# Forty-five column-reordering copies moved from GpSimd to ScalarE, with a newly written instruction order

## The chip, the cores and the metric

The kernel runs on one core of a Trainium2 chip. The metric is the device time of one execution in microseconds (us). The kernel before took 771.58 us as the median of three runs, which lay between 764.45 and 779.27 us.

A core has five instruction queues that run beside each other and meet only at semaphores: TensorE (PE in the profile, with its weight loads as PEld), VectorE (DVE), ScalarE (ACT), GpSimd (POOL) and SyncE (SP), which here does nothing but issue DMA transfers. Each queue runs its instructions strictly in the order in which they were written.

## The reference

Two blocks follow each other. The first is a linear-attention recurrence over 768 steps, for 4 batches of 8 heads with 40 channels each; the second is a dense layer pair over the resulting 3072 tokens, with an activation h·cos(h) between the two products.

```python
def _attn_ref(r, k, v, w, a, b):
    ...
    for t in range(S):
        ...
        y[:, :, t] = np.einsum('bhd,bhde->bhe', rt, state)
        Sa = np.einsum('bhde,bhe->bhd', state, at)
        state_decay = state * wt[:, :, None, :] - np.einsum('bhd,bhe->bhde', Sa, bt)
        state = state_decay + np.einsum('bhd,bhe->bhde', vt, kt)

def _moe_ref(x, w_in, w_out):          # x: 3072 x 320, w_in: 320 x 2048
    h = x @ w_in
    g = h * np.cos(h)
    return (g @ w_out).astype(np.float32)
```

## The kernel before

**Attention.** The 768 steps are cut into 24 chunks of 32 steps. Within a chunk the recurrence is turned into small matrix products plus the inverse of a triangular 32x32 matrix per batch and head. Four chunks share one inversion, so there are six inversions ("quads" 0 to 5). An inversion is a run of short VectorE steps: for quads 2 to 5 each step j is one multiply into `inv_tmp` (line 655) and one subtract into `inv` (line 659), 31 steps a quad; it starts with a transpose into `u` (line 647) and ends with a transpose into `rt` (line 663). The state is carried from chunk to chunk through the tokens t, q, x, s and z (functions `ch_t` to `ch_z`); in `ch_z` VectorE adds the products to the state `qz` (line 916) and GpSimd multiplies it by the decay (line 917).

**Dense layers.** Finished chunks are joined in pairs to 12 groups of 256 tokens. For each group and each of four blocks j of the inner dimension, `first_a` and `first_b` fill two PSUM tiles `ph` with x·w_in. For each of the two, ScalarE rounds (line 1000), VectorE subtracts (line 1002), ScalarE takes the absolute value and the sine (lines 1006, 1007) and VectorE multiplies (line 1010). From group 3 on the second product is done with seven instead of eight block products: small sums on GpSimd (`s`, lines 1082 and 1090) and VectorE (lines 1084, 1086), then `seven`.

**The copies.** The operands r, v, a and w are wanted with the channels on the partitions. For early chunks TensorE transposes them. From quad 3 on for w, and from quad 2 on for a, r and v, it is done by way of DRAM: `quad_fetch` (line 277) brings four chunks of one operand into the tile `ws` with four DMAs; for w, VectorE then forms running products in place (lines 357 and 362); `quad_turn` (line 291) copies the columns of `ws` from the order (t, d) to (d, t) in three parts of 14, 13 and 13 channels, that is 448, 416 and 416 elements a partition; `quad_store` (line 298) writes each part to DRAM; `turned_load` (line 322) reads it back with the channels on the partitions. There are 15 such operands (four each of a, r and v, three of w), so 45 copies. There is one `ws`, so the next fetch waits for the third copy of the operand before. The copies' targets are two buffers used in turn (`nat_a`), so a copy also waits until the store of the part two before it has landed.

**Order.** Nothing is scheduled automatically. The string `PLAN` holds 1,536 tokens, each the name of a function above and its arguments, and the instructions are emitted in that order; each queue gets its part of it. `rf:a:3` is the fetch of operand a for quad 3 (for w the token is `sf:3`, and `sc:3` and `ss:3` are its running product and the store of it), `pt:a:3:1` the copy of its part 1, `st:a:3:1` the store of that part, `lt:12:a` the load of chunk 12. `ij:12:20` is step 20 of the inversion of the quad that starts at chunk 12, `fa:g:j` and `fb:g:j` are the first product of group g and block j, `y:g:j:n` the rest of its activation. `L:c:n:q:h` are the first loads with the queue that issues them (s, a or p for SyncE, ScalarE or GpSimd). `B:n` and `K:n` put in n matmuls on a zero tile.

Of the kernel before, what the change touches and what calls it, by code (L numbers as in the profile page):

```python
# [17 lines left out]
L:1:a:p:l L:2:w:s:l L:0:w:a:r L:0:b:p:r L:1:b:s:r L:0:v:p:r B:4 L:0:a:p:r B:5 B:3 L:3:w:s:r L:1:w:s:l  # L18
L:1:w:a:r L:0:w:s:l L:3:b:p:r L:2:b:s:r L:3:w:s:l L:0:a:s:l L:0:k:s:r L:3:a:s:r L:1:a:p:r L:0:b:p:l L:2:b:s:l
pw:0 L:2:w:s:r L:2:a:p:r L:0:r:s:r L:1:b:s:l L:2:a:p:l pa:0 L:3:b:p:l pw:2 L:3:a:s:l pa:2 sp:0 sf:1 pb:0 pn:0  # L20
L:0:k:s:l sc:1 pb:2 pn:2 lo:2 L:0:v:s:l B:4 lo:0 kn:0 is:0 wf:1 L:0:r:s:l in:0 L:1:r:p:l L:1:k:p:r L:1:k:s:l
ip:0:15 wt:1 ip:0:14 ld:5:a ip:0:13 ip:0:12 ip:0:11 ip:0:10 ip:0:9 k:0 L:1:r:s:r v:0 L:1:v:p:l B:2 ip:0:8
ip:0:7 ip:0:6 g:0 ip:0:5 ip:0:4 L:1:v:s:r wf:0 B:4 wf:2 kn:1 k:1 in:1 B:3 v:1 L:2:r:s:r ip:0:3 ip:0:2 x:0 g:1
ip:0:1 L:2:v:s:r wt:2 L:2:k:p:r wm:1 wg:1 it:0 L:2:v:s:l ss:1 wp:1 ih:0 F:0:0:0 S:0:0:0 wm:2 wg:2 wf:3 wt:3
ld:4:w wp:2 wf:4 s:0 L:2:r:p:l K:6 ld:5:w wg:3 wt:0 wm:0 B:4 wf:6 wg:0 in:2 z:0 L:2:k:s:l kn:2 B:5 wm:3 wp:3
L:3:v:p:l B:4 wf:7 F:0:1:0 t:1 B:5 L:3:v:p:r wp:0 K:14 wt:4 wm:4 F:0:2:0 L:3:k:p:r wt:6 wm:6 q:1 L:3:r:s:l
wf:8 wg:4 wp:4 wt:7 k:2 wm:7 wf:9 wg:6 wp:6 wg:7 B:4 L:3:r:s:r wp:7 S:0:1:0 wf:10 K:6 x:1 wt:8 B:3 B:3 wt:9
wm:9 L:3:k:p:l wf:5 s:1 B:4 v:2 wm:8 wg:9 wp:9 g:2 wg:8 wp:8 B:6 tk:0 wt:10 wm:10 z:1 wg:10 wp:10 B:6 t:2 q:2
wf:11 wf:12 wt:11 tk:1 K:4 wf:13 wm:11 wt:5 wm:5 wg:5 wp:5 kn:3 B:3 S:0:2:0 wg:11 k:3 wp:11 wt:13 wm:13 B:6
x:2 tb:0 in:3 v:3 wg:13 wt:12 wm:12 wp:13 tb:1 wg:12 wf:14 wt:14 K:6 wp:12 fa:0:0 fb:0:0 y:0:0:0 y:0:0:1 wg:14  # L30
y:0:0:2 wm:14 s:2 K:29 wf:16 wf:15 ld:4:r g:3 wp:14 fa:0:1 fb:0:1 ld:4:b wf:17 F:0:3:1 wt:15 wm:15 wg:15 r:4
sd:0:0:0 z:2 y:0:1:1 ld:5:b sd:0:0:1 K:13 y:0:1:0 y:0:1:2 S:0:3:1 sf:2 ld:4:v wt:16 wm:16 ld:4:a ld:6:b t:3
K:20 r:5 wp:15 wf:18 sc:2 wg:16 sd:0:1:1 pw:4 ld:7:w fa:0:2 q:3 wp:16 fb:0:2 y:0:2:0 pa:4 ld:6:w wf:19 y:0:2:1
in:4 ld:4:k kn:4 tk:2 wt:17 wm:17 x:3 pb:4 y:0:2:2 sd:0:1:0 wg:17 ss:2 s:3 ld:7:b sd:0:2:1 wp:17 wt:18 wm:18
wt:19 wm:19 ld:5:k wg:19 fa:0:3 r:7 ld:6:a r:6 pn:4 lo:4 pw:6 fb:0:3 z:3 pb:6 y:0:3:0 ld:7:a pa:6 rf:a:2
y:0:3:2 wg:18 sp:4 pn:6 sd:0:2:0 wp:18 is:4 ip:4:15 lo:6 ld:5:r v:4 pt:a:2:1 y:0:3:1 wp:19 k:4 ip:4:14 t:4 g:4
ip:4:13 ip:4:12 ip:4:11 tb:2 ip:4:10 ip:4:9 ip:4:8 pt:a:2:0 ip:4:7 tk:3 ip:4:6 ip:4:5 ip:4:4 ld:5:v in:5
sd:0:3:0 kn:5 k:5 q:4 ip:4:3 ip:4:2 v:5 tb:3 fa:1:0 g:5 st:a:2:0 pt:a:2:2 ld:9:w rf:r:2 ip:4:1 fb:1:0 y:1:0:0
st:a:2:1 pt:r:2:1 T:1:0 x:4 sd:0:3:1 st:a:2:2 y:1:0:1 pt:r:2:0 it:4 F:4:0:1 y:1:0:2 F:4:1:1 sd:1:0:0 ld:9:b
ld:8:w lt:8:a ld:8:b ih:4 S:4:0:1 st:r:2:0 s:4 st:r:2:1 r:9 lt:9:a ld:6:k fa:1:1 pw:8 xa:8 ld:11:w ld:6:v r:8  # L40
ld:10:w fb:1:1 z:4 kn:6 ld:11:b T:0:0 sd:1:0:1 y:1:1:1 pb:8 y:1:1:0 y:1:1:2 F:4:3:1 pt:r:2:2 rf:v:2 st:r:2:2
ld:6:r F:4:2:1 t:5 fa:1:2 tk:4 lt:10:a S:4:1:1 q:5 ld:10:b fb:1:2 xa:9 in:6 y:1:2:0 ld:7:k x:5 lt:11:a
sd:1:1:0 s:5 k:6 pt:v:2:0 r:11 sp:8 y:1:2:1 sd:1:1:1 pt:v:2:1 pn:8 y:1:2:2 sd:1:2:1 z:5 o:0:0 ld:7:v tk:5
fa:1:3 v:6 pw:10 xa:10 st:v:2:0 pt:v:2:2 tb:4 g:6 r:10 fb:1:3 ld:7:r in:7 y:1:3:0 y:1:3:1 S:4:3:1 xa:11
sd:1:2:0 tb:5 pb:10 S:4:2:1 y:1:3:2 o:0:1 pn:10 is:8 sf:3 t:6 ij:8:31 fa:2:0 sc:3 kn:7 k:7 q:6 v:7 ij:8:30
st:v:2:2 fb:2:0 y:2:0:1 x:6 sd:1:3:0 sd:1:3:1 ij:8:29 ij:8:28 ij:8:27 ij:8:26 st:v:2:1 ss:3 y:2:0:0 lt:8:r
ld:12:b y:2:0:2 ij:8:25 ld:12:w ld:13:w s:6 pt:w:3:0 st:w:3:0 lt:8:v fa:2:1 fb:2:1 z:6 y:2:1:1 ij:8:24
sd:2:0:0 sd:2:0:1 T:0:1 y:2:1:0 y:2:1:2 T:3:0 o:1:0 r:12 tk:6 g:7 ld:8:v ld:8:k ij:8:23 ij:8:22 t:7 fa:2:2
ij:8:21 q:7 o:1:1 pt:w:3:2 fb:2:2 x:7 T:0:2 T:0:3 y:2:2:1 lt:9:r pt:w:3:1 st:w:3:2 ij:8:20 ij:8:19 y:2:2:0
kn:8 y:2:2:2 sd:2:1:0 k:8 st:w:3:1 s:7 ld:9:k sd:2:1:1 ij:8:18 ij:8:17 ij:8:16 z:7 ij:8:15 ij:8:14 rf:a:3  # L50
# [78 lines left out]
def kernel(  # L129
# [43 lines left out]
    nc = tc.nc  # L173
# [1057 lines left out]
```

## Time and profile before

| | |
|---|---|
| median of three runs | 771.58 us |
| profiled execution, its own time | 774.15 us |
| its span, first to last instruction | 772.4 us |
| mean granted clock of TensorE | 0.971 |
| moved by DMA | 78.12 MB, 101 GB/s on average |

The profile is that of one execution, and the prediction's sum starts from that execution's own time: 772.4 us of span and 1.75 us around it. An engine's busy time is the time in which one of its instructions ran. A row of the groups names the line, the engine, the operation, the tiles written and read, the shape and the count; then stand the busy time of the group in us and the mean of one in ns; then the time that the engine sat idle just before these instructions, with what ended most of it. The chain of waits is followed back from the last instruction to what released each one; its shares tell which engine the time went through.

### The profile page before, as it was taken

To read this page: it belongs to the slowest core of one execution; us is meant where nothing else is said; L and a number is where in the kernel's file an instruction comes from. 1 tells how busy PE (TensorE), PEld (TensorE's weight loads), DVE (VectorE), ACT (ScalarE), POOL (GpSimd) and SP (SyncE) were. 2 spreads that over 40 slices of the span, in tenths; PEclk is the share of its full clock that TensorE was granted. 3 is DMA by queue.
4 is the path that set the end of the run, shared out by engine and by line. 5 is a ranking of instruction groups with operands and counts; after the bars stand their busy time and mean duration, and the time that the engine had idled before them with its cause. 6 is when DMAs were issued, how large, how long until landed. Compare 5 with 4: busy or idle time off the path is not lost.

```text
span 772.4 us, 40189 instructions
## 1 busy us (share of the span) xinstructions
PE 713.3 (92%) x17948; PEld 586.3 (76%) x17948; DVE 558.7 (72%) x1199; ACT 359.3 (47%) x719; POOL 291.3 (38%) x468
## 2 busy tenths in 40 slices
PE   4758999999989998999998999999999999999995
PEld 2645678777777776888877888887888888888885
DVE  5989889896346898387998768898647895454342
ACT  1335565754544534354444454535445445554432
POOL 8625303333340553463463442532624313231211
PEclk9869999999998998999999999999999999999998
DMA  8576564565555368446567566556633221211000
GB/s 129 103 178 170 148 174 100 133 122 87 109 125 114 74 129 140 95 93 138 96 134 132 120 129 128 122 121 105 131 76 68 53 58 48 49 27 30 21 18 18
DMA packets 268541, 78.12 MB, mean 101 GB/s; under 512 B 230128, under 2 KB 261872, under 8 KB 268368
## 3 DMA queue, kind: packets, MB, share of 16 engines
q1 hardware_dynamic: 266064, 73.82, 46.0%
q8 instruction: 141, 2.31, 1.3%
q0 software_dynamic: 1216, 1.56, 1.1%
q10 hardware_dynamic: 1088, 0.16, 0.1%
q14 instruction: 32, 0.26, 0.1%
HBM read 54.53 MB, written 20.97 MB: 98 GB/s over the span
## 4 chain that ended last, share of the span: by engine, by line
PE 64%; DVE 22%; ACT 5%; issue 4%; SPq 2%; POOL 2%; DMA 1%; DVEq 0%; POOLq 0%
PE ph L210 22%; PE po L210 15%; PE dps L210 4%; DVE inv L659 3%; PE x0ps L210 3%; DVE inv_tmp L655 3%; PE p L210 2%; PE sps L210 2%; PE gram L210 2%; PE busy L210 2%; DVE turns L1002 2%; PE qps L210 2%; PE nps L210 2%; PE sT L807 1%; DVE gT L1010 1%
## 5 line engine op out<-in xcount | busy, mean ns | idle before, releaser
L210 PE MATMUL ph<-xT,w_in_sb 128*128 128x256 f32 x768 | 186.4, 389 | 2.6 <-DVE gT L1010 2.0
L210 PEld LDWEIGHTS ph<-xT,w_in_sb 128*128 128x128 f32 x768 | 141.6, 192 | 31.4 <-issue 12.6
L210 PE MATMUL po<-w_out_sb,gT 128*128 128x160 f32 (+1 forms) x624 | 132.7, 351 | 1.4 <-DVE gT L1010 1.2
L1000 ACT ACTIVATE turns<-ph,few 128x512 f32<-128x512 f32 x96 | 63.6, 686 | 126.6 <-PE ph L210 124.7
L210 PEld LDWEIGHTS po<-w_out_sb,gT 128*128 128x128 f32 x624 | 98.5, 193 | 19.4 <-DVE gT L1010 2.5
L1002 DVE SCALAR_TENSOR_TENSOR turns<-turns,ph 128x512 f32<-128x512 f32 x96 | 62.7, 680 | 67.0 <-ACT turns L1000 66.6
L917 POOL TENSOR_TENSOR qz<-qz,wc 128x160 f32<-128x160 f32 x92 | 40.0, 458 | 119.4 <-DVE qz L916 119.4
L1010 DVE TENSOR_TENSOR gT<-ph,turns 128x512 f32<-128x512 f32 x96 | 64.6, 682 | 25.3 <-ACT turns L1007 25.2
L1007 ACT ACTIVATE turns<-turns,few 128x512 f32<-128x512 f32 x96 | 69.3, 722 | 3.1
L1006 ACT ACTIVATE turns<-turns 128x512 f32<-128x512 f32 x96 | 60.2, 627 | 20.6 <-DVE turns L1002 20.4
L1090 POOL TENSOR_TENSOR s<-gT 128x256 f32<-128x256 f32 x36 | 27.5, 763 | 111.7 <-DVE gT L1086 111.7
L291 POOL COPY nat_a<-ws 128x416 f32<-128x416 f32 (+1 forms) x45 | 48.0, 1075 | 52.3 <-DVE ws L362 18.0
L659 DVE TENSOR_TENSOR inv<-inv,inv_tmp 128x31 f32<-128x31 f32 (+15 forms) x124 | 60.3, 487 | 4.3
L655 DVE TENSOR_TENSOR inv_tmp<-u,inv 128x31 f32<-128x31 f32 (+15 forms) x124 | 54.2, 437 | 2.4
L210 PE MATMUL po<-TW,gT 128*128 128x160 f32 x288 | 52.8, 307 | 1.8 <-DVE gT L1086 1.7
L210 PE MATMUL ph<-xT,w_in_tail 64*128 64x256 f32 (+1 forms) x456 | 54.4, 396 | 0.0
L1082 POOL TENSOR_TENSOR s<-gT 128x256 f32<-128x256 f32 x36 | 27.7, 769 | 56.9 <-DVE gT L1010 53.0
L210 PEld LDWEIGHTS po<-TW,gT 128*128 128x128 f32 x288 | 43.9, 194 | 3.3 <-DVE gT L1086 3.2
L825 ACT COPY qz<-qps 40x256 f32<-40x256 f32 x92 | 33.7, 367 | 23.2 <-PE qps L210 21.8
L565 DVE RECIPROCAL rw<-nat_w 128x320 f32<-128x320 f32 x20 | 42.7, 2140 | 0.0
L210 PEld LDWEIGHTS ph<-xT,w_in_tail 64*128 64x128 f32 (+1 forms) x456 | 32.3, 169 | 11.1 <-issue 7.0
L566 POOL TENSOR_TENSOR bn<-nat_b,rw 128x320 f32<-128x320 f32 x22 | 19.7, 896 | 52.6 <-DVE rw L565 40.7
(157 smaller groups left out, 1260.2 us busy)
## 6 DMA issues: line engine op xcount, KB each, us to landing
words<-in_moe_w_in_dram SPq DMA_DIRECT2D x8, 512.0 KB
xd<-yt SPq DMA_DIRECT2D x48, 80.0 KB
out_dram<-ot SPq DMA_DIRECT2D x24, 160.0 KB
nat_k<-in_k_dram SPq DMA_DIRECT2D x88, 40.0 KB
nat_v<-in_v_dram SPq DMA_DIRECT2D x88, 40.0 KB
nat_b<-in_b_dram SPq DMA_DIRECT2D x84, 40.0 KB
wd<-ws SPq DMA_DIRECT2D x5, 640.0 KB
nat_w<-wd SPq DMA_DIRECT2D x80, 40.0 KB
```

Of the source, the lines that this page charges most:

```text
L210: nc.tensor.matmul(o, lhsT=lhsT, rhs=rhs, start=start, stop=stop, skip_group_check=True)
L291: nc.gpsimd.tensor_copy(quad_part(n, q, i).rearrange("p (d t) -> p d t", t=C), ws[:, :, PARTS[i]].rearrange("p t d -> p d t"))
L565: nc.vector.reciprocal(rw, wn)
L655: nc.vector.tensor_tensor(tmp, u[:, j : j + 1, :j].to_broadcast([P, C - j, j]), x[:, j:, j : j + 1].to_broadcast([P, C - j, j]), ALU.mult,)
L659: nc.vector.tensor_tensor(x[:, j:, :j], x[:, j:, :j], tmp, ALU.subtract)
L825: nc.scalar.copy(pick(qz[rows], f * (NZ - C), (NZ, 2 * B), (1, C)), ps[f][rows, : 2 * B * C].rearrange("p (i t) -> p i t", t=C),)
L917: nc.gpsimd.tensor_tensor(z, z, wc.rearrange("p (b f m) -> p f m b" if re_laid("w", c // 4) else "p (f m b) -> p f m b", f=2, m=2)[:, :, : ...
L1000: nc.scalar.activation(t, u, ACTF.Identity, bias=rnd, scale=1.0)
L1002: nc.vector.scalar_tensor_tensor(t, t, -ROUND, u, ALU.add, ALU.subtract)
L1006: nc.scalar.activation(t, t, ACTF.Abs)
L1007: nc.scalar.activation(t, t, ACTF.Sin, bias=half_pi, scale=-2.0 * math.pi)
L1010: nc.vector.tensor_tensor(gT[:, 2 * e : 2 * e + 2, :n], phs[e], ns[e].rearrange("p (f t) -> p f t", f=2), ALU.mult)
```

## The change

`quad_turn` does its copy with `nc.scalar.copy` in place of `nc.gpsimd.tensor_copy`; the operands are the same.

```diff
     def quad_turn(n, q, i):
-        nc.gpsimd.tensor_copy(
+        nc.scalar.copy(
             quad_part(n, q, i).rearrange("p (d t) -> p d t", t=C), ws[:, :, PARTS[i]].rearrange("p t d -> p d t")
         )
```

`PLAN` is written anew. It has 1,536 tokens as before. The counts of the filler matmuls are unchanged (78 by `B`, 98 by `K`, 60 by `P`). Only the first loads differ as a set: of 48, the new one issues 25 from SyncE, 21 from GpSimd and 2 from ScalarE, where it was 27, 19 and 2. All else is a matter of places: TensorE's own order stays nearly the same, while copies, stores, fetches, loads, inversion steps and activation steps move by some tokens against each other. Around the operands a and r of quad 3, for instance:

```diff
...
-sd:2:1:1 ij:8:18 ij:8:17 ij:8:16 z:7 ij:8:15 ij:8:14 rf:a:3
-pt:a:3:1 pt:a:3:0 ld:13:b ld:9:v kn:9 lt:12:w fa:2:3 r:13 fb:2:3 sd:2:2:1 T:1:1 g:8 tk:7 ij:8:13 y:2:3:1
-ij:8:12 tb:6 ij:8:11 y:2:3:0 st:a:3:0 tb:7 t:8 ld:15:w pt:a:3:2 rf:r:3 T:2:0 sd:2:2:0 q:8 y:2:3:2 st:a:3:2
-T:2:1 pt:r:3:0 lt:10:r ij:8:10 ld:10:k st:a:3:1 pt:r:3:1 ij:8:9 ij:8:8 ij:8:7 ij:8:6 ij:8:5 ij:8:4 k:9 pb:12
...
+y:2:2:2 s:7 ij:8:18 ij:8:17 ij:8:16 sd:2:1:1 tb:6 lt:8:r rf:a:3 z:7 pt:a:3:0 pt:a:3:1 ld:9:v lt:8:v r:13
+fa:2:3 lt:12:w st:a:3:0 pt:a:3:2 lt:9:r g:8 o:1:0 T:1:1 T:1:2 ld:9:k kn:9 fb:2:3 sd:2:2:0 ij:8:15 ij:8:14
+ij:8:13 ij:8:12 st:a:3:1 y:2:3:1 t:8 tk:7 T:2:0 ld:10:k ij:8:11 y:2:3:0 tb:7 k:9 y:2:3:2 ij:8:10 q:8 o:1:1
+ij:8:9 ld:10:v ij:8:8 ij:8:7 st:a:3:2 ij:8:6 ij:8:5 ij:8:4 rf:r:3 lt:9:v sd:2:2:1 ij:8:3 ld:14:b lt:13:w
+ij:8:2 fa:3:0 fb:3:0 lt:10:r x:8 lt:12:a ij:8:1 ie:8 sd:2:3:1 y:3:0:1 u:3:0:0 y:3:0:0 pt:r:3:1 xw:12 xw:13
+T:2:1 pt:r:3:0 sd:2:3:0 y:3:0:2 st:r:3:0 s:8 ld:14:w u:3:0:1 pb:12 st:r:3:1 pt:r:3:2 m:3:0:0 u:3:0:2 fa:3:1
...
```

More of the change, by code (lines that the diff above doesn't have):

```diff
@@ L23 @@
[L23 to L37, printed above, removed]
@@ new lines @@
+ip:0:15 ip:0:14 ip:0:13 ip:0:12 ip:0:11 ip:0:10 ip:0:9 ip:0:8 B:2 v:0 B:3 g:0 L:1:r:p:r B:4 ip:0:7 ld:5:a
+L:1:k:s:l ip:0:6 L:1:v:p:l L:1:v:s:r kn:1 k:1 L:1:r:s:l in:1 v:1 L:2:v:p:r wm:1 ss:1 ld:4:b ip:0:5 ip:0:4
+ip:0:3 L:2:k:s:l x:0 ip:0:2 ip:0:1 it:0 g:1 L:2:r:p:r ih:0 wf:2 wg:1 wp:1 L:2:r:p:l F:0:0:0 L:2:v:p:l wt:2
+S:0:0:0 wm:2 F:0:2:0 wf:3 wg:2 wp:2 wf:6 ld:4:w in:2 s:0 wt:3 wm:3 wt:0 wm:0 K:6 wg:3 B:4 z:0 wf:4 wp:3 wg:0
+wp:0 B:4 L:2:k:s:r kn:2 B:3 K:14 F:0:1:0 wf:8 wt:4 wf:7 t:1 wt:6 wm:4 wm:6 B:5 S:0:1:0 B:5 wg:4 wg:6 q:1
@@ new lines @@
+ij:12:20 ij:12:19 o:3:1 ij:12:18 ij:12:17 ij:12:16 ij:12:15 m:4:1:1 lt:12:v z:11 u:4:1:3 fa:4:3 fb:4:3
+st:a:4:0 y:4:3:1 k:12 m:4:2:0 u:4:2:0 lt:13:r u:4:2:1 u:4:2:2 t:12 ij:12:14 ld:13:v ld:13:k kn:13 lt:16:w
+pt:a:4:2 g:12 ij:12:13 ij:12:12 pb:16 tk:11 m:4:2:1 u:4:3:0 y:4:3:0 y:4:3:2 u:4:3:1 q:12 u:4:2:3 m:4:3:0
+ij:12:11 u:4:3:2 ij:12:10 ij:12:9 ij:12:8 m:4:3:1 ij:12:7 ij:12:6 st:a:4:1 st:a:4:2 tb:11 ij:12:5 lt:13:v
+ij:12:4 ij:12:3 c:4:0 rf:r:4 ld:19:w lt:16:a lt:17:w k:13 xw:16 ld:14:k x:12 ij:12:2 u:4:3:3 pt:r:4:1 c:4:1
@@ new lines @@
+kn:19 u:7:3:3 ms:7 y:8:0:1 y:8:0:2 ij:20:28 s:18 c:7:2 ij:20:27 k:19 ij:20:26 st:v:5:1 ld:20:k lt:21:r
+ij:20:25 u:8:0:0 ij:20:24 fa:8:1 u:8:0:1 z:18 ld:20:v fb:8:1 lt:19:v g:19 kn:20 t:19 st:v:5:2 m:8:0:0 ij:20:23
+u:8:0:2 ld:21:k ij:20:22 ij:20:21 lt:20:v q:19 y:8:1:0 tk:18 y:8:1:2 ld:21:v k:20 m:8:0:1 y:8:1:1 lt:20:r
+ij:20:20 x:19 o:7:0 ij:20:19 m:8:1:0 u:8:1:0 u:8:1:1 u:8:1:2 u:8:0:3 u:8:1:3 ij:20:18 ij:20:17 fa:8:2 ij:20:16
+s:19 fb:8:2 tb:18 z:19 y:8:2:1 m:8:1:1 y:8:2:0 y:8:2:2 o:7:1 tk:19 tb:19 t:20 ij:20:15 ij:20:14 fa:8:3
```

163 lines of the change are left out of this document (80 added, 83 removed).

## Prediction

> **What bounds the kernel now.** I read the page's busy times first, then the chain of waits, then busy times by stage, and last the order of time around the copies.
>
> ```profile
> span 772.4 us, 40189 instructions
> ...
> PE 713.3 (92%) x17948; PEld 586.3 (76%) x17948; DVE 558.7 (72%) x1199; ACT 359.3 (47%) x719; POOL 291.3 (38%) x468
> ...
> PE 64%; DVE 22%; ACT 5%; issue 4%; SPq 2%; POOL 2%; DMA 1%; DVEq 0%; POOLq 0%
> PE ph L210 22%; PE po L210 15%; PE dps L210 4%; DVE inv L659 3%; PE x0ps L210 3%; DVE inv_tmp L655 3%; PE p L210 2%; PE sps L210 2%; PE gram L210 2%; PE busy L210 2%; DVE turns L1002 2%; PE qps L210 2%; PE nps L210 2%; PE sT L807 1%; DVE gT L1010 1%
> ```
>
> TensorE is busy for 92% of the span and carries 64% of the chain. VectorE carries 22%, of which the inversion steps (3% and 3%) are the largest single part. ScalarE and GpSimd, between which the copies move, carry 5% and 2%. So the change works through what it does to TensorE's and VectorE's waits. The stages tell how much there is to win:
>
> ```profile
> 0.00:60.00 60.00, 36.14 (x1019) 26.74 (x1023) 48.44 (x99) 16.99 (x39) 32.91 (x82) 0.83 0.68 134
> 60.00:100.00 40.00, 35.50 (x1120) 24.20 (x1112) 35.14 (x74) 21.94 (x44) 17.14 (x24) 0.96 0.59 162
> 100.00:600.00 500.00, 478.89 (x12626) 395.93 (x12625) 383.33 (x813) 244.98 (x496) 202.10 (x305) 0.98 0.57 115
> ```
>
> The columns after the window and its length are the busy times of PE, PEld, DVE, ACT and POOL. From 100 to 600 us, where all copies lie, TensorE idles for 500 - 478.9 = 21.1 us; in the first 60 us, before any copy, for 23.9 us. Whatever the change mends between 100 and 600 us can therefore give at most 21 us, and it has no such limit downwards.
>
> **What leaves GpSimd.** The copies do not stand on the chain, but they hold VectorE up. This stretch of the order of time shows it (start, duration, engine, line, tiles):
>
> ```profile
> 294.96 0.32 DVE L655 TENSOR_TENSOR inv_tmp<-u,inv 128x156 f32<-128x156 f32 x1
> 294.99 1.20 POOL L291 COPY nat_a<-ws 128x448 f32<-128x448 f32 x1 [6.23 <-DMA nat_k<-in_k_dram]
> ...
> 295.31 1.06 DVE L659 TENSOR_TENSOR inv<-inv,inv_tmp 128x156 f32<-128x156 f32 x1
> ...
> 297.70 0.25 DVE L655 TENSOR_TENSOR inv_tmp<-u,inv 128x87 f32<-128x87 f32 x1
> 297.83 0.99 POOL L291 COPY nat_a<-ws 128x416 f32<-128x416 f32 x1 [1.65 <-DMA wda<-nat_a]
> 297.98 0.94 DVE L659 TENSOR_TENSOR inv<-inv,inv_tmp 128x87 f32<-128x87 f32 x1
> ...
> 304.06 0.43 DVE L851 COPY x<-x0ps 128x288 f32<-128x288 f32 x1
> ...
> 304.77 0.50 PE L210 MATMUL sps<-x,rt 32*32 32x72 f32 x16 [3.44 <-ACT x L850]
> ```
>
> A step on 156 elements takes 0.32 us alone and 1.06 us when a copy runs beside it; one on 87 elements 0.25 and 0.94 us; each ends with the copy. The copy of `x0ps` (line 851) is queued behind this inversion, and TensorE stands for 3.44 us there, the longest gap past the start. How much the steps lose in all follows from their own groups:
>
> ```profile
> L659 DVE TENSOR_TENSOR inv<-inv,inv_tmp 128x31 f32<-128x31 f32 (+15 forms) x124 | 60.3, 487 | 4.3
> L655 DVE TENSOR_TENSOR inv_tmp<-u,inv 128x31 f32<-128x31 f32 (+15 forms) x124 | 54.2, 437 | 2.4
> ...
> L655 DVE TENSOR_TENSOR inv_tmp<-u,inv 128x256 f32<-128x256 f32 x4 | 1.7, 422 | 0.1
> L655 DVE TENSOR_TENSOR inv_tmp<-u,inv 128x31 f32<-128x31 f32 x8 | 1.6, 199 | 0.2
> ```
>
> The last two are free of such stretching: (422 - 199) / (256 - 31) = 0.99 ns an element, and 199 - 31 x 0.99 = 168 ns fixed. The 31 steps of an inversion have j(32 - j) elements, 5,456 in sum, so four inversions should take 124 x 0.168 + 21,824 x 0.00099 = 42.5 us on each line, 85 us on both. They take 114.5. GpSimd as a whole costs the inversions 29.5 us. The copies' share is bounded by these sums over the four stretches in which the inversions run (225 to 315, 345 to 420, 465 to 540 and 585 to 645 us), first of all work, then of line 291 alone:
>
> ```profile
> 345.00:420.00 75.00, 71.13 (x1683) 60.81 (x1684) 67.11 (x147) 31.83 (x67) 31.68 (x43) 0.98 0.60 122
> ...
> sum 300.00, PE 284.73 PEld 236.64 DVE 253.19 ACT 134.01 POOL 108.32; mean PE 71.18 PEld 59.16 DVE 63.30 ACT 33.50 POOL 27.08
> ```
> ```profile
> 225.00:315.00 90.00, 9.86 (x9) 0.92 0.61 120
> 345.00:420.00 75.00, 10.34 (x10) 0.98 0.60 122
> 465.00:540.00 75.00, 8.30 (x8) 1.00 0.61 120
> ...
> sum 300.00, POOL 28.49; mean POOL 7.12
> ```
>
> By share of GpSimd's time the copies take 28.5 / 108.3 = 26% of 29.5, or 7.8 us. If each of the 27 copies there holds one step for 1.06 - 0.32 = 0.74 us, it is 20 us. I take 13, near the middle: the rows above show full blocking, but not every copy meets a step. The two lines give about 6% of the span to the chain, 46 of their 114.5 us, so 40% of this reaches the end: **-5 us** (-3 to -8).
>
> GpSimd's queue is also 48 us shorter, by the row below. At its rate on the chain, 2% of 772.4 = 15.4 of 291.3 busy us, that is 48 x 0.053 = **-2.5 us**. Who gains are the sums `s` and the decay of `qz`, which queue behind copies.
>
> **What ScalarE takes on.** The trace has no ScalarE copy that reads with a large step, so the cost is bounded by its nearest rows:
>
> ```profile
> L291 POOL COPY nat_a<-ws 128x416 f32<-128x416 f32 (+1 forms) x45 | 48.0, 1075 | 52.3 <-DVE ws L362 18.0
> ```
> ```profile
> L811 ACT COPY s<-sT 104x416 f32<-104x416 f32 x46 | 21.3, 509 | 17.4 <-PE sT L807 17.4
> ...
> L625 ACT COPY nt<-nps 128x256 f32<-128x256 f32 x24 | 12.8, 637 | 23.3 <-PE nps L210 23.3
> ...
> L632 ACT COPY noff<-nps 128x256 f32<-128x256 f32 x8 | 2.6, 399 | 0.0
> ```
>
> Line 811 copies 416 elements in unbroken runs in 0.51 us. Lines 625 and 632 copy the same 256 elements, the first writing each one 128 bytes from the last: 238 ns more, 0.93 ns an element. The new copies read with a step of 160 bytes. If reading costs as writing does, one takes 0.51 + 416 x 0.00093 = 0.90 us, and 45 of them 41 us; at the other end 23 us. I take 41, since the stepped row is the nearer one. At ScalarE's rate on the chain, 5% of 772.4 = 38.6 of 359.3 busy us or 0.107, that is **+4.4 us** (+2.5 at the low end).
>
> [...]
>
> The larger question is waiting. On GpSimd a copy could wait at no cost:
>
> ```profile
> L291 POOL COPY nat_a<-ws x45: 982/1047/1253, 156.7 to 580.0; 128x416 f32<-128x416 f32 x30, 128x448 f32<-128x448 f32 x15
> ...
> its engine sat idle before it (us, times) until:
>   DVE ws L362: 18.0, 2
>   DMA wda<-nat_a: 10.3, 3
>   DMA wdv<-nat_a: 9.9, 2
>   DMA nat_k<-in_k_dram: 6.2, 1
> ```
>
> GpSimd idled for 52.3 us ahead of copies, for running products, stores and fetches. On ScalarE whatever stands behind a copy waits too: by the new order mostly the evictions of `gram`, `sT`, `sps` and the rounding of `ph`, each of which TensorE needs back. The new order keeps most waits short. I counted TensorE's work between tokens, with the mean durations of its groups in this trace, as a rough clock. Copies of an operand stand in ones and twos, some 1 to 25 us after their fetch by that clock, and the third copy is often 7 us or more behind the first, whose store must land before it. Three places look tight: `pt:a:3:2` and `pt:r:3:2` come about 2 to 3.5 us by it after the first copy, and `pt:a:2:0` directly follows its fetch. What landing takes shows here:
>
> ```profile
> 287.91 1.79 SPq L277 DMA_DIRECT2D ws<-in_r_dram  x4
> ```
> ```profile
> 294.49 0.46 SPq L298 DMA_DIRECT2D wda<-nat_a  x1
> ```
>
> The fetch's issues ended near 289.7 and its first copy ran at 294.99, 5.3 us on; the store issued at 294.49 released the copy at 297.83, 3.3 us on. Waiting lies between 0 and the old 52 us. I take 10 us, three tight places at about 3.3 us; as a standing engine holds up all behind it, I charge 30% rather than 11%: **+3 us**.
>
> **Front.** The new first loads move two more transfers to GpSimd. Nothing in the profile says whether the first 100 us get better or worse; I take 0 and allow 4 us both ways.
>
> **Sum.** -5 - 2.5 + 4.4 + 3 + 0 = 0 against the profiled run's 774.15 us. That run lies 0.3% above the median of 771.58, so 774.15 x 771.58 / 774.15 is again about **772 us**.
>
> **Rivals.**
>
> *ScalarE becomes the wait: slower.* If ScalarE stands ahead of copies as long as GpSimd did, the copies cost it 52 + 41 = 93 us in the stretch where it is the hand between TensorE's banks. For it: 15 operands each need a fetch to land first, and TensorE has only two `ph` tiles to run ahead with. Against it: ScalarE is idle for half the stage (245 of 500 us busy) and the order puts most copies into gaps. At the same 30%, 28 - 7.5 = +20 gives 794 us, or 792 on the median's footing. It decides from 22% on: (13 + 7.5) / 93 reaches 2%, twice ScalarE's present rate.
>
> *VectorE's relief is worth more: faster.* If the copies' full 20 us leave the inversions, which run while VectorE is 67.1 of 75 us busy, and most of TensorE's 21.1 us of idle time goes, -18 gives 756, and a better front 752 us. For it: the 3.44 us gap above, which two copies helped to make. Against it: nearly all of 21 us would have to go.
>
> *VectorE isn't relieved at all:* other GpSimd work, which makes up 74% of its time there, slides into the freed places. Then the -7.5 us go and 779 us result, still within 2%.
>
> **How the numbers follow.** Little changes 0.36 (with the last rival in it, 762 to 783 us), slower through ScalarE's waits 0.34, faster through VectorE 0.30. Two per cent, 756 and 787 us, is about what a measurement of this kernel can tell from no change, as its three runs spread by 1.9%. Both signs hold most of the chance, so the range takes in the two centres, 752 and 792, and 5 us more at the open, upper end: 752 to 797 us.
>
> **What would show it.** Right: the inversion lines fall from 114.5 us to about 101, line 291 stands under ACT at about 0.9 us, ScalarE's busy time is near 400 us, and idle time ahead of line 291 is about 10 us. Wrong towards slower: that idle time is above 30 us, or TensorE's idle time between 100 and 600 us is above 35 us with ScalarE as its releaser. Wrong towards faster: that idle time is under 8 us. If the first 60 us differ by over 4 us, the front decided.

## The result and the profile after

The changed kernel took 760.88 us (median of 20 runs, 755.39 to 765.81), the kernel before beside it 768.38 us (20 runs, 760.23 to 779.27). The ratio is 0.9914 with a 95% interval of 0.9886 to 0.9943: a gain of 0.9%, small but outside the scatter, where no net change was forecast. The profiled execution of the changed kernel took 755.39 us, its fastest, and that of before 774.15 us, one of its slower ones. So the two profiles show 18.7 us of difference, of which the medians bear out 7.5. Ratios and intervals leave out the executions over 1.5% above the fastest of their kernel in the same series; where a reading hangs on that, the ratio of the means of all executions stands beside it.

The busy times, the clock and the chain from the page of the changed kernel:

```profile
span 753.7 us, 40220 instructions
...
PE 702.8 (93%) x17956; PEld 578.2 (77%) x17956; DVE 534.8 (71%) x1199; ACT 398.0 (53%) x764; POOL 245.8 (33%) x427
...
PE 69%; DVE 13%; ACT 5%; DMA 4%; SPq 4%; issue 3%; POOL 1%; DVEq 0%; POOLq 0%; ACTq 0%
...
L291 ACT COPY nat_a<-ws 128x416 f32<-128x416 f32 (+1 forms) x45 | 45.1, 1019 | 16.9 <-DMA wdv<-nat_a 5.7
L659 DVE TENSOR_TENSOR inv<-inv,inv_tmp 128x31 f32<-128x31 f32 (+15 forms) x124 | 50.0, 404 | 4.2
...
L655 DVE TENSOR_TENSOR inv_tmp<-u,inv 128x31 f32<-128x31 f32 (+15 forms) x124 | 46.5, 375 | 2.7
```

The copies stand under ACT now, with the 45 us they cost there. VectorE's share of the chain fell from 22% to 13%, and the two inversion lines from 114.5 to 96.5 us. The same two steps that took 1.06 and 0.94 us beside a copy run free; this is the order of time on VectorE in the changed kernel:

```profile
286.30 0.32 DVE L655 TENSOR_TENSOR inv_tmp<-u,inv 128x156 f32<-128x156 f32 x1
286.66 0.32 DVE L659 TENSOR_TENSOR inv<-inv,inv_tmp 128x156 f32<-128x156 f32 x1
...
288.59 0.25 DVE L659 TENSOR_TENSOR inv<-inv,inv_tmp 128x87 f32<-128x87 f32 x1
```

Where the time came from shows in the busy times by stage (columns as before: PE, PEld, DVE, ACT, POOL, then the clock), first of the changed kernel, then two short stretches of the kernel before:

```profile
0.00:60.00 60.00, 36.44 (x1029) 25.73 (x1031) 49.06 (x99) 18.01 (x41) 35.51 (x86) 0.83 0.68 141
60.00:100.00 40.00, 35.32 (x1126) 24.70 (x1107) 35.96 (x76) 21.11 (x42) 17.19 (x24) 1.00 0.59 161
100.00:600.00 500.00, 486.86 (x13093) 403.66 (x13095) 373.40 (x847) 292.92 (x558) 160.66 (x270) 1.00 0.58 117
220.00:240.00 20.00, 19.58 (x536) 15.49 (x533) 14.62 (x33) 14.11 (x28) 4.41 (x9) 1.00 0.64 144
300.00:320.00 20.00, 19.76 (x596) 16.88 (x596) 11.58 (x25) 12.76 (x24) 8.66 (x14) 1.00 0.68 132
```
```profile
220.00:240.00 20.00, 17.90 (x388) 14.35 (x386) 12.77 (x24) 10.09 (x20) 4.93 (x7) 0.83 0.60 130
300.00:320.00 20.00, 16.33 (x376) 13.53 (x376) 11.47 (x28) 8.51 (x17) 4.49 (x11) 0.83 0.63 118
```

Between 100 and 600 us TensorE's idle time fell from 21.1 to 500 - 486.9 = 13.1 us. Two short stretches hold 1.7 + 3.4 = 5.1 of these 8.0 us, the second of them the 3.44 us gap that the prediction showed. Over the whole span 8.2 us of idle time went. The other 10.5 of the 18.7 us are TensorE's own busy time, 713.3 before and 702.8 after for the same matmuls: its clock stood at 0.83 in those two stretches and at 1.00 after. The first 60 us are as they were.

The busy time should not be put down to the change as it stands. The changed kernel was profiled a second time, in an execution of 766.63 us:

```profile
100.00:600.00 500.00, 485.60 (x12874) 402.54 (x12872) 369.25 (x836) 291.16 (x551) 154.28 (x262) 0.99 0.58 118
```

Here TensorE idled for 14.4 us between 100 and 600 us, 6.7 less than before, but it was busy for 711.9 us over the span, only 1.4 less than before; its clock was lower in the first 60 us, 0.78 against 0.83. So both profiles bear out 6.7 to 8.0 us of idle time, about the 7.5 us of the medians, and most of the 10.5 us differs from one execution to the next.

### The profile page after: what moved, and what is told of

Its sections match the earlier page's. It is cut to its first block, busy times and chain, and to the rows that moved or that the text cites. A ratio compares the mean times of both kernels' runs of the same rounds, so it can differ in the third digit from the quotient of the medians.

```text
span 753.7 us, 40220 instructions
## 1 busy us (share of the span) xinstructions
PE 702.8 (93%) x17956; PEld 578.2 (77%) x17956; DVE 534.8 (71%) x1199; ACT 398.0 (53%) x764; POOL 245.8 (33%) x427
## 4 chain that ended last, share of the span: by engine, by line
PE 69%; DVE 13%; ACT 5%; DMA 4%; SPq 4%; issue 3%; POOL 1%; DVEq 0%; POOLq 0%; ACTq 0%
PE ph L210 28%; PE po L210 17%; PE dps L210 4%; PE x0ps L210 4%; PE gram L210 3%; PE p L210 3%; SPq L262 2%; PE sps L210 2%; PE qps L210 2%; DVE inv L659 2%; PE nps L210 2%; DVE inv_tmp L655 2%; DVE gT L1010 2%; PE sT L807 1%; DMA nat_v<-in_v_dram 1%
## 5 line engine op out<-in xcount | busy, mean ns | idle before, releaser
L210 PE MATMUL ph<-xT,w_in_sb 128*128 128x256 f32 x768 | 184.3, 386 | 2.5 <-issue 1.0
L210 PEld LDWEIGHTS ph<-xT,w_in_sb 128*128 128x128 f32 x768 | 139.8, 190 | 31.1 <-issue 12.0
L210 PE MATMUL po<-w_out_sb,gT 128*128 128x160 f32 (+1 forms) x624 | 130.3, 347 | 3.0 <-DVE gT L1010 2.3
L1010 DVE TENSOR_TENSOR gT<-ph,turns 128x512 f32<-128x512 f32 x96 | 64.4, 684 | 21.1 <-ACT turns L1007 20.8
L1006 ACT ACTIVATE turns<-turns 128x512 f32<-128x512 f32 x96 | 60.1, 626 | 12.4 <-DVE turns L1002 12.3
L291 ACT COPY nat_a<-ws 128x416 f32<-128x416 f32 (+1 forms) x45 | 45.1, 1019 | 16.9 <-DMA wdv<-nat_a 5.7
L659 DVE TENSOR_TENSOR inv<-inv,inv_tmp 128x31 f32<-128x31 f32 (+15 forms) x124 | 50.0, 404 | 4.2
L655 DVE TENSOR_TENSOR inv_tmp<-u,inv 128x31 f32<-128x31 f32 (+15 forms) x124 | 46.5, 375 | 2.7
L916 DVE TENSOR_TENSOR qz<-dps,qz 128x160 f32<-128x160 f32 x92 | 29.2, 317 | 16.8 <-PE dps L210 16.8
```

The lines of the kernel that those rows point to most:

```text
L210: nc.tensor.matmul(o, lhsT=lhsT, rhs=rhs, start=start, stop=stop, skip_group_check=True)
L291: nc.scalar.copy(quad_part(n, q, i).rearrange("p (d t) -> p d t", t=C), ws[:, :, PARTS[i]].rearrange("p t d -> p d t"))
L655: nc.vector.tensor_tensor(tmp, u[:, j : j + 1, :j].to_broadcast([P, C - j, j]), x[:, j:, j : j + 1].to_broadcast([P, C - j, j]), ALU.mult,)
L659: nc.vector.tensor_tensor(x[:, j:, :j], x[:, j:, :j], tmp, ALU.subtract)
L1006: nc.scalar.activation(t, t, ACTF.Abs)
L1010: nc.vector.tensor_tensor(gT[:, 2 * e : 2 * e + 2, :n], phs[e], ns[e].rearrange("p (f t) -> p f t", f=2), ALU.mult)
```

## The experiments

Each ratio is to the kernel before on the same chip, with its 95% interval. "Old order" is the `PLAN` of before, "new order" the changed one; where line numbers differ by a few, the edit made the file longer.

### The two halves by themselves

The changed engine without the changed order, and the other way round:

```diff
 # before, with its own PLAN
-        nc.gpsimd.tensor_copy(
+        nc.scalar.copy(
```

> The written order of before, the 45 copies on ScalarE. The changed kernel took 0.9914 of the time of before. If the relief of VectorE does it (the copies no longer hold inversion steps), nearly all of that is here already: ratio 0.990 to 0.996, and lines 655 and 659 together fall from 114.5 us to about 97. If the new order does it, the ratio is 1.00 or above, because ScalarE now stands at waits that the old order left to GpSimd: idle time ahead of line 291 above 30 us, ratio 1.00 to 1.02.

```diff
 # after, with its own PLAN
-        nc.scalar.copy(
+        nc.gpsimd.tensor_copy(
```

> The written order of the changed kernel, the 45 copies on GpSimd as before. If the relief of VectorE does it, the gain is gone: ratio 0.998 to 1.01, lines 655 and 659 together above 108 us. If the new order does it, the ratio is near 0.991 with those lines still near 114 us.

Measured: old order on ScalarE 1.0107 (1.0056 to 1.0158), new order on GpSimd 1.0072 (1.0036 to 1.0108). Both halves are slower alone and the two together are faster, at 0.9914. No sum over the parts of this change, each priced alone, can give that. The two inversion lines stood at 99.7 and 108.8 us: on ScalarE the old order relieved VectorE too, and the kernel was slower all the same.

What goes wrong in the old order on ScalarE is to be seen around 220 us. First the waits of line 291 in that run, then the order of time there, one engine below the other:

```profile
L291 ACT COPY nat_a<-ws x45: 985/1004/1075, 157.0 to 590.0; 128x416 f32<-128x416 f32 x30, 128x448 f32<-128x448 f32 x15
...
  DMA wda<-nat_a: 17.1, 5
  DMA wdv<-nat_a: 11.9, 2
  DMA ws<-in_a_dram: 6.8, 1
```
```profile
226.38 1.00 ACT L291 COPY nat_a<-ws 128x416 f32<-128x416 f32 x1 [8.18 <-DMA wdv<-nat_a]
227.29 0.43 ACT L786 COPY vvm<-gram 128x128 f32<-128x128 f32 x2
...
227.58 0.29 DVE L781 TENSOR_TENSOR ag<-gram,su 128x128 f32<-128x128 f32 x1 [8.48 <-ACT vvm L786]
...
228.18 2.14 DVE L565 RECIPROCAL rw<-nat_w 128x320 f32<-128x320 f32 x1
...
230.41 0.86 POOL L566 TENSOR_TENSOR bn<-nat_b,rw 128x320 f32<-128x320 f32 x1 [11.26 <-DVE rw L565]
...
231.32 1.97 PE L521 MATMUL bT<-ident,bn 128*128 128x128 f32 x8 [6.68 <-POOL bn L566]
```

ScalarE stands 8.18 us for the store of the part two before. The eviction into `vvm` is queued behind it, VectorE stands 8.48 us for that, VectorE's reciprocal stands behind that, GpSimd's `bn` waits for the reciprocal, and TensorE for `bn`: four engines for one store. TensorE's own wait names GpSimd as its releaser; only the chain, followed back, leads to the copy. ScalarE's idle time ahead of copies is 44.5 us in this run, 16.9 in the changed kernel.

### VectorE's relief alone

In the old order, GpSimd keeps its place and its queue, but hardly reads while it works: two memsets of the target and a copy of one channel. Then without the memsets.

```diff
-        nc.gpsimd.tensor_copy(
-            quad_part(n, q, i).rearrange("p (d t) -> p d t", t=C), ws[:, :, PARTS[i]].rearrange("p t d -> p d t")
-        )
+        for _ in range(2):                      # this loop not in the second run
+            nc.gpsimd.memset(quad_part(n, q, i), 0.0)
+        nc.gpsimd.tensor_copy(quad_part(n, q, i)[:, :C], ws[:, :, PARTS[i].start])
```

> The order of before; in place of each copy GpSimd does two memsets of its target and then copies one channel (32 of 416 or 448 elements), so the reordering of the other channels is left out. GpSimd is busy as long as before, about 1.0 us a copy, but reads SBUF for a small part of that only. If GpSimd's reading of SBUF is what holds VectorE, lines 655 and 659 fall to about 100 us and the ratio is 0.990 to 0.996, as with the copies gone. If it is GpSimd's occupied queue (the sums and the decay behind the copies) that costs, the ratio is 0.998 to 1.002 with those lines at whatever value.

> The order of before; each copy on GpSimd moves one channel only, the rest of the reordering is left out. All waits, stores and loads stay. This is the most that taking the copies off GpSimd can give in the old order. VectorE's relief alone: lines 655 and 659 near 100 us, ratio 0.988 to 0.995, and no better than the run with memsets by more than 0.003. If GpSimd's queue matters too, better than the run with memsets by over 0.003. If neither is on the path, 0.998 to 1.002.

Measured: 0.9871 (0.9819 to 0.9923) with the memsets, 0.9922 (0.9883 to 0.9961) without. The groups of the run with memsets:

```profile
L661 DVE TENSOR_TENSOR inv<-inv,inv_tmp 128x31 f32<-128x31 f32 (+15 forms) x124 | 51.2, 413 | 4.3
L657 DVE TENSOR_TENSOR inv_tmp<-u,inv 128x31 f32<-128x31 f32 (+15 forms) x124 | 48.2, 388 | 2.4
L292 POOL MEMSET nat_a<- 128x416 f32 (+1 forms) x90 | 40.9, 454 | 47.7 <-DMA wda<-nat_a 23.2 <-DMA wdv<-nat_a 15.8 <-DMA wdw<-nat_a 3.3
```

GpSimd is busy with 41 us of memsets and stands 47.7 us ahead of them, yet the inversion lines come down to 99.4 us and the time by 1.3%. So it is the copies' reading that holds VectorE, and taking it away is worth 0.8 to 1.3% with the order untouched (0.6 to 0.9% with all executions counted). The length of GpSimd's queue shows no effect. VectorE and GpSimd met here, then, not only at semaphores: a step on 156 elements took 1.06 us beside a copy that reads SBUF and 0.32 us alone, and the two inversion lines took 99.4 us with memsets, which only write, against 114.5 us with whole copies. The run with memsets in the new order, below, shows it on a single step: one on 31 elements, at 415.34 us, took 0.21 us while GpSimd did a memset, and one at 299.74 us, with GpSimd idle, 0.21 us as well.

### ScalarE's work and its waits

The copies cut to one channel on ScalarE, in both orders:

```diff
-            quad_part(n, q, i).rearrange("p (d t) -> p d t", t=C), ws[:, :, PARTS[i]].rearrange("p t d -> p d t")
+            quad_part(n, q, i)[:, :C], ws[:, :, PARTS[i].start]
```

> The changed kernel, but each ScalarE copy moves one channel only (the reordering of the other channels is left out); all waits stay. It measures what the 45 copies' own time on ScalarE costs in the new order: about 45 x 0.75 = 34 us less ScalarE work. If the new order hides that work (my reading now), the ratio to before is 0.988 to 0.994, as with the full copies at 0.9914. If the work costs at ScalarE's rate on the chain, as the prediction charged it (+4.4 us), the ratio is about 0.986 or below.

> The order of before with ScalarE copies of one channel only (the reordering of the others is left out). ScalarE keeps its waits (44.5 us ahead of the copies with full ones) and loses 34 us of work. If the waits are what makes the old order slow on ScalarE (1.0107 with full copies), it stays above 1.003 with idle time ahead of line 291 near 45 us. If the work itself does it, it falls to 0.99, where VectorE's relief stands alone.

Measured: new order 0.9821 (0.9776 to 0.9866), old order 1.0083 (1.0040 to 1.0125). In the old order, 11 us of copying instead of 46 changes the time by less than the intervals, 1.0107 against 1.0083. ScalarE still stands as long, mostly for the stores:

```profile
L291 ACT COPY nat_a<-ws 128x32 f32<-128x32 f32 x45 | 11.0, 251 | 48.3 <-DMA wda<-nat_a 18.7 <-DMA wdv<-nat_a 13.5 <-DMA ws<-in_a_dram 5.7
```

The waits may cover the copying there; the intervals leave room for a cost of up to 0.9%. In the new order the 45 us seem to cost 0.9%, 0.9821 against 0.9914, but these two ratios were taken apart from each other (with all executions counted they are 0.987 and 0.989); side by side it came out smaller as well:

> The changed kernel itself, on the same chip as the next three, so that they can be compared with it: ratio 0.988 to 0.995 as before.

> The changed kernel with ScalarE copies of one channel (the reordering of the others is left out), beside the changed kernel on the same chip. Apart they gave 0.9821 and 0.9914. If the copies' own time on ScalarE is on the path in the new order, this is 0.004 to 0.010 below the changed kernel; if the new order hides it, within 0.003 of it.

Measured: the changed kernel again 0.9891 (0.9808 to 0.9973), with one channel 0.9855 (0.9759 to 0.9951). The difference of 0.4% is inside the scatter. The copying costs somewhere from nothing to 0.9%.

### The new order on GpSimd without the reading copies

```diff
 # after
-        nc.scalar.copy( ... )
+        for _ in range(2):
+            nc.gpsimd.memset(quad_part(n, q, i), 0.0)
+        nc.gpsimd.tensor_copy(quad_part(n, q, i)[:, :C], ws[:, :, PARTS[i].start])
```

> The order of the changed kernel on GpSimd, with two memsets and a copy of one channel in place of each copy (the reordering of the other channels is left out). GpSimd as busy as with full copies, but hardly reading. With full copies the new order on GpSimd has 1.0072. If that is VectorE being held, the ratio falls by about what it fell in the old order (0.013), to 0.990 to 0.997, near the changed kernel's 0.9914. If it is the new order that leaves GpSimd's other work too late, it stays at 1.003 to 1.008.

Measured: 1.0030 (0.9992 to 1.0068), at the lower edge of what the second theory gave. Without the reading copies the new order is still not faster on GpSimd. GpSimd stands in this order too:

```profile
L292 POOL MEMSET nat_a<- 128x416 f32 (+1 forms) x90 | 40.8, 453 | 47.8 <-DMA wdv<-nat_a 28.8 <-DMA wda<-nat_a 7.5 <-DMA wdr<-nat_a 7.0
```

It stood as long in the old order with memsets (47.7 us), which was the fastest of all in that order. So the length of GpSimd's standing does not decide. That it is what stands behind it is argued here, not shown by this run.

### Another move of the same kind

The copies of v in line 742 and their fellows, which the plan can put on either engine, also moved to ScalarE, with the new order else unchanged:

```diff
-kn:0 ... kn:23
+ka:0 ... ka:23
```

> A try for a faster kernel: the changed kernel with the 24 copies of v into its tile (line 742, 0.54 us each on GpSimd, reading SBUF) also on ScalarE, the order untouched. If relief of VectorE is all, a further 0.001 to 0.003 faster than 0.9914. If an engine change without its own order costs through ScalarE's waits for the v loads, as it did in the old order, slower than the changed kernel: 0.995 to 1.01.

Measured: 1.0017 (0.9974 to 1.0060), 1% slower than the changed kernel, though the inversion lines stay at 96.1 us. ScalarE now stands for fetches of v at places that were written for GpSimd, and TensorE behind it (ScalarE, then TensorE):

```profile
422.77 0.46 ACT L742 COPY vvm<-nat_v 128x320 f32<-128x320 f32 x1 [7.31 <-DMA nat_v<-in_v_dram]
...
424.42 0.89 ACT L811 COPY s<-sT 104x416 f32<-104x416 f32 x2
...
416.59 0.88 PE L807 MATMUL sT<-ident,qz 104*104 104x104 f32 x8
424.96 1.28 PE L210 MATMUL qps<-rT,s 40*40 40x32 f32 x59 [7.49 <-ACT s L811]
```

### A third buffer

If the stores are what the copies wait for, a third target buffer (`rp`, free from quad 3 on) should end most of it:

```diff
-        at_i = nat["a", (3 * (4 * q + "avrw".index(n)) + i) % 2].rearrange("p h d -> p (h d)")
+        at = 3 * (4 * q + "avrw".index(n)) + i
+        if q > 2:
+            at = 3 * (4 * q + "wavr".index(n)) + i
+        t = rp if q > 2 and at % 3 == 2 else nat["a", at % 3 if q > 2 else at % 2]
+        at_i = t.rearrange("p h d -> p (h d)")
```

> The order of before with the copies on ScalarE, and from quad 3 on a third buffer for their results (the tile rp, which nothing uses any more by then), so that a copy no longer waits for the store just before the last. If ScalarE's standing at stores is what costs in the old order, idle time ahead of line 291 falls from 44.5 us to about 25 us and the ratio from 1.0107 to about 1.000; the long gap at the third copy of v in quad 2, which still has two buffers, stays. If the order costs for another reason, the ratio stays above 1.006.

> The changed kernel with the same third buffer: a try for a faster one. Of its 16.9 us of idle time ahead of line 291, some 7 us are stores from quad 3 on. If ScalarE's standing there is on the path, 0.002 to 0.005 below the changed kernel; if the new order has it hidden, the same within 0.003.

Measured, both with the copies on ScalarE: old order 1.0204 (1.0125 to 1.0284), a miss; new order 0.9871 (0.9816 to 0.9926), the same as the 0.9891 beside it. In the old order the idle time fell only from 44.5 to 37.4 us, since the same copies then waited for their fetch:

```profile
L295 ACT COPY nat_a<-ws 128x416 f32<-128x416 f32 (+1 forms) x33 | 33.7, 1030 | 37.4 <-DMA ws<-in_r_dram 10.8 <-DMA wdv<-nat_a 7.9 <-DMA ws<-in_a_dram 7.4
```

So the stores are not the cause by themselves: these copies are written too soon after all that they need. That the kernel became slower still is not shown: with all executions counted the ratios are 1.011 here and 1.016 with two buffers.

### Copies moved in either order

Ten copies of the old order that stood on ScalarE, and one fetch, moved some tokens later; and five copies of the new order moved up close to their store or fetch. Two of the moves of each:

```diff
 # old order, ScalarE
-st:v:2:0 pt:v:2:2 tb:4 g:6 r:10 fb:1:3 ld:7:r in:7 y:1:3:0 y:1:3:1 S:4:3:1 xa:11
+st:v:2:0 tb:4 g:6 r:10 fb:1:3 ld:7:r in:7 y:1:3:0 y:1:3:1 S:4:3:1 xa:11 pt:v:2:2
...
 # new order, ScalarE
-rf:r:4 ld:19:w lt:16:a lt:17:w k:13 xw:16 ld:14:k x:12 ij:12:2 u:4:3:3 pt:r:4:1
+rf:r:4 pt:r:4:1 pt:r:4:0 ld:19:w lt:16:a lt:17:w k:13 xw:16 ld:14:k x:12 ij:12:2 u:4:3:3
```

> The old order with the copies on ScalarE, in which only ten copies that stood, and one fetch, are moved some tokens later: v of quad 2 parts 0 and 2, all three of a of quad 3 with the fetch of r behind them, r of quad 3 parts 0 and 1, v of quad 3 part 2, r of quad 4 part 0 and w of quad 5 part 2. Everything else of the old order stays. Theory, that standing copies are what makes the old order slow on ScalarE: idle time ahead of the copies falls from 44.5 us to 15 to 22, the two gaps of TensorE of 4 to 7 us near 225 and 303 us go, and the time against the kernel before falls from 1.011 to 0.990 to 0.998. Rival, that the rest of the new order (loads, inversion steps, activation steps) is what helps: the idle time falls but the ratio stays at 1.005 or above. If the idle time does not fall below 30 us the edit did not do its work and nothing follows.

> The mirror: the changed kernel, in which five copies stand as close to their store or fetch as in the old order: v of quad 2 part 2 right behind the store of part 0, and parts 0 and 1 of r of quads 3 and 4 right behind their fetch. Everything else of the new order stays. Theory, that the waits of a few copies decide: idle time ahead of the copies rises from 16.9 us (13.4 in its second run) to 30 to 40, TensorE gets gaps of 4 to 7 us near 215 and 285 us, and the ratio rises from 0.990 to between 1.000 and 1.010. Rival, that the rest of the new order helps: the ratio stays below 0.995.

Measured: old order with later copies 1.0083 (1.0042 to 1.0124), new order with earlier ones 0.9994 (0.9957 to 1.0032). The second goes most of the way that the theory gave: five copies put back cost 0.8%, most of the gain, though the idle time ahead of copies rose to 23.8 us only, not to 30. One of them, with what stands behind it (ScalarE, then TensorE):

```profile
216.79 1.00 ACT L300 COPY nat_a<-ws 128x416 f32<-128x416 f32 x1 [5.74 <-DMA wdv<-nat_a]
217.69 1.01 ACT L634 COPY nt<-nps 128x256 f32<-128x256 f32 x2
...
218.32 0.90 PE L219 MATMUL gram<-aT,kT 40*32 40x32 f32 x34 [4.65 <-ACT nt L634]
```

The first goes the rival's way: the idle time fell to 12.4 us, below that of the changed kernel, and the two long gaps near 225 and 303 us are gone, but the time hardly moved by these ratios; with all executions counted it came from 1.016 to 1.004, short of the theory's 0.998 all the same. So the copies' places are needed for the gain and do not suffice for it. Two more runs of this moved order, one with a single channel a copy and one with whole copies on GpSimd, ask what is left:

> The old order with the ten copies moved later, each copy on ScalarE for one channel only (the reordering of the other channels is left out). Now ScalarE has neither the 45 us of copying nor the long waits, and GpSimd does not hold VectorE. Theory, that what is left of the old order's loss on ScalarE is the copying itself, in places where ScalarE has no gap for it: the ratio falls from 1.008 to 0.985 to 0.996, as with one channel on GpSimd (0.992). Rival, that the moves themselves cost, as stores, fetches and turned loads come later behind them: the ratio stays at 1.003 or above though ScalarE does almost nothing for the copies.

> The same old order with the ten copies moved later, but with whole copies on GpSimd as in the kernel before. If the moves cost by themselves, the ratio is 1.005 to 1.015, since only the places differ from the kernel before. If they cost nothing and ScalarE's copying is the loss, it is 0.995 to 1.003.

Measured: one channel 1.0006 (0.9978 to 1.0035), whole copies on GpSimd 0.9967 (0.9914 to 1.0020), or 0.999 with all executions counted. The moves by themselves show no cost. The copying costs about 1.0083 - 1.0006 = 0.8% here, or 0.4% with all executions counted. That leaves 1.0006 against the 0.9922 of one channel on GpSimd, another 0.8%, with neither copies on GpSimd nor much copying on ScalarE, though with 12.8 us of idle time ahead of ScalarE's copies: what else of the old order does not suit ScalarE is open.

One candidate stands in the traces and was not tried. The stores are issued from SyncE, whose queue is in order too: it stands at a store until the copy is done, and the loads written behind the store wait with it. In the kernel before it stands 5.9 us for the copy that ends at 541.95 us; the store is issued at 541.98 and the load of `vp` behind it at 542.78 us. The waits of SyncE at line 298 for the copies, before, in the old order on ScalarE and in the changed kernel (us in all, times, longest):

```profile
SPq L298 <- POOL nat_a L291: 11.0, 4, 5.9
...
SPq L298 <- ACT nat_a L291: 31.2, 9, 9.5
...
SPq L298 <- ACT nat_a L291: 4.8, 3, 3.5
```

Added up over all that it waited for at the stores, SyncE stood 19 us before, 45 in the old order on ScalarE, 48 there with the third buffer, 35 with later copies, 27 with later copies of one channel, 8 with one channel on GpSimd, and 15 in the changed kernel. It also parts the two runs with memsets, in which GpSimd stood equally long: 14 us in the old order, 37 in the new. The run with five copies put back does not fit, with 15 us and most of the gain gone. No run moves the stores alone, so whether this standing costs the time or only goes with it is open.

## Why the prediction was wrong

**The forecast**, 772 us and no net change, was off by more than the scatter: a gain of 0.9%, which on the forecast's footing is 771.58 x 0.9914 = 765 us, where the sum gave 0. That lies inside the 762 to 783 us given for little change and inside the range, but the runs tell it from no change, and the sum has to account for 7 us. None of the signs named for being wrong showed: idle time was 16.9 us ahead of the copies and 13.1 us on TensorE, neither above 30 nor under 8. They watched single terms, and it was the sum that failed.

**VectorE's relief (-5): right in mechanism, if anything too small.** The inversion lines fell by 18.0 us, not 13, to 96.5 instead of 101, but not all of it came from the engine. With the order held, leaving GpSimd took 14.8 us off in the old order (to 99.7) and 12.3 in the new one (from 108.8), close to the 13; the rest came with the order. Another VectorE line gained that the prediction did not count, the sum of line 1084, from 605 to 463 ns each; before, then after:

```profile
L1084 DVE TENSOR_TENSOR gT<-gT 128x256 f32<-128x256 f32 x36 | 21.8, 605 | 10.0 <-POOL s L1082 9.0
```
```profile
L1084 DVE TENSOR_TENSOR gT<-gT 128x256 f32<-128x256 f32 x36 | 16.7, 463 | 7.0 <-POOL s L1082 6.4
```

The new order on GpSimd has 18.8 us on this line, so of its 5.1 us some 3 came with the order as well. By the runs with memsets and with one channel, the relief is worth 0.8 to 1.3%, 6 to 10 us, or 5 to 7 us with all executions counted: the 5 us forecast stand at the lower edge.

**GpSimd's shorter queue (-2.5): not shown.** The memsets kept the queue full and the gain stayed. The two gain terms together, 7.5 us, are about what the relief alone gives.

**ScalarE's work (+4.4): within what the runs allow.** A copy took 1.02 us, above the 0.90 taken as the upper end, and ScalarE's busy time is 398 us as forecast. What that costs was 0.4 to 0.8% (3 to 6 us) in the moved old order, and nothing to 0.9% in the new one.

**ScalarE's waits (+3): more idle time, at less cost.** It was 16.9 us, not 10 (13.4 in the second profile). Its remaining cost could not be found: the third buffer took it from the 13.4 us of the run beside it to 10.6 and the time stayed, which is a weak test.

**The step that failed** is the sum, "-5 - 2.5 + 4.4 + 3 + 0 = 0". It priced work and waits on ScalarE at rates, 11% from the old chain and 30% chosen, as if a microsecond cost the same wherever it is written, and let the new order count only through the lengths of waits and the first loads. Measured against the relief alone (one channel on GpSimd, old order), ScalarE with the old order costs 1.0107 - 0.9922, 1.85% or 14 us; with the new order 0.9914 - 0.9922, nothing that shows, the intervals leaving room for 3 us. The forecast's 7.4 us (4.4 and 3) fits neither. These differences hold ScalarE and the order together: what the copying still costs in the new order, the order must give back elsewhere. The front was rightly put at 0 as far as its busy times show; the order behind it was not.

**The rivals.** "ScalarE becomes the wait" describes the old order on ScalarE: 44.5 us of idle time where 52 were assumed, but 1.1% slower, not 2.6%. The new order keeps it off, and putting five copies back takes most of the gain away. The rate of 22% from which it was to decide should be 25%: two per cent is 15.4 us, and (15.4 + 7.5) / 93 = 25%. "VectorE's relief is worth more" has the right mechanism and sign; its 18 us were more than twice what came, as it let nearly all of TensorE's 21.1 us of idle time go, and 6.7 to 8.0 went. "VectorE isn't relieved" fell with the inversion lines.

**Open:** which other part of the new order is needed. Stores, loads, inversion steps and activation steps all moved, and they were not tried one at a time; the stores on SyncE's queue are the first to try.

## What to carry to other kernels

When work moves to another in-order queue, price it together with its place: list for each moved instruction what it waits for and which instructions stand behind it, and follow those over all engines to the one that bounds. The same copies on the same engine were 1.1% slower or 0.9% faster by the order alone, so testing an engine change with the old order can reject a good change, and testing a new order on the old engine as well. Length of waiting is a poor measure: GpSimd stood 47.7 us at no loss in one order, and in another 47.8 us with the gain gone.

## What was not expected of the hardware

**Some gaps cost more than their length.** In the kernel before, TensorE's clock stood at 0.50 right after gaps of 2.10 and 3.44 us, which end at 229.37 and 304.77 us, and 2 us after one of 1.58 us, which ends at 350.32; after two of 1.36 us, which end at 422.32 and 516.58 us, it stayed at 1.00. Old order on ScalarE, around the 6.68 us gap, and the kernel before, around the gap of 2.10 us:

```profile
215.00:223.00 8.00, 8.00 (x231) 6.62 (x230) 1.47 (x5) 2.06 (x4) 3.46 (x8) 1.00 0.56 102
223.00:231.00 8.00, 1.64 (x7) 0.81 (x5) 3.42 (x6) 2.60 (x6) 0.59 (x1) 0.77 0.55 114
231.00:239.00 8.00, 7.68 (x213) 6.89 (x214) 4.93 (x10) 5.35 (x10) 2.28 (x5) 0.50 0.78 157
```
```profile
222.00:230.00 8.00, 5.90 (x234) 4.52 (x237) 4.21 (x8) 4.35 (x7) 3.88 (x6) 0.93 0.49 117
230.00:238.00 8.00, 8.00 (x159) 6.90 (x150) 5.84 (x14) 3.45 (x8) 0.41 (x1) 0.64 0.60 100
```

From 231 to 239 us, after the long gap, the clock was 0.50, which loses up to 4 us more, an estimate from half of these 8 us; after the short one the mean clock was 0.64: in steps of 2 us it was 0.50 from 229.4 to 235.4 us and 1.00 from 237.4 us on. Length alone does not tell which gap does it. With later whole copies on GpSimd, where the mean clock was 1.00 from 100 to 600 us, the eight `po` matmuls behind a gap of 2.03 us that ends at 296.35 us took 1.35 us; eight of the same shape at a clock of 0.50, behind the 3.44 us gap of the kernel before, took 2.50 us. Yet in that kernel 0.50 followed the shorter gap of 1.58 us. Just ahead of the 2.10 us gap stood small matmuls (`below` with 32*32, `nps` with 40*32); whether they have a part in it is not shown. A matmul of `ph` with 256 columns took 634 ns at a clock of 0.50 in the kernel before (from 309.3 us) and 379 ns at 1.00 (from 310.9 us). In this way idle time saved can bring down the busy time of the same matmuls too; how much of the difference in busy time, 10.5 us in the first profile of the changed kernel and 1.4 us in the second, comes from that is not shown.

**A stepped read on ScalarE.** The two shapes of the copy, and the unbroken copy of line 811, in the changed kernel:

```profile
L291 ACT COPY nat_a<-ws 128x416 f32<-128x416 f32 x30 | 29.9, 999 | 10.7 <-DMA wdv<-nat_a 4.5 <-DMA wda<-nat_a 2.5 <-DMA wdr<-nat_a 2.2
L811 ACT COPY s<-sT 104x416 f32<-104x416 f32 x46 | 21.2, 509 | 12.4 <-PE sT L807 12.4
...
L291 ACT COPY nat_a<-ws 128x448 f32<-128x448 f32 x15 | 15.9, 1061 | 6.3 <-DMA ws<-in_v_dram 3.9 <-DMA wdv<-nat_a 1.2 <-DMA ws<-in_a_dram 1.1
```

With a step of 160 bytes 416 elements take 1.00 us instead of 0.51, and 32 more elements 62 ns, 1.9 ns each. Line 811 reads PSUM, so the step is not the only difference; but line 1006 reads SBUF without a step and takes 0.63 us for 512 elements. The prediction's 0.90 us, carried over from a stepped write, was too low: over both shapes a copy took 1.02 us, about as long as on GpSimd (1.08 us).
